# Ten dk stores that leave out one DMA engine, in place of eight that leave out two

## The chip, the core and the metric

The kernel runs on one core of a Trainium2 chip. The time is that of one launch on the device in microseconds (us), median of several runs. A ratio of two kernels is of their fast runs (in brackets its 95% interval); it isn't quite the ratio of the medians that stand beside it. The kernel before was timed anew in each set of rounds: 1280.82 to 1284.12 us median, single runs 1278.9 to 1287.4. The first four experiments ran on one chip and the other eight on another; where the text compares kernels of the two, the kernel before differs by 1.5 us between them (1280.82 and 1282.27).

## The reference

Attention of one query row per head, forward and backward: 64 heads (2 x 32), 8192 keys, head width 128, bf16.

```python
def _fwd_reference(q, k, v):
    scale = q.shape[-1] ** -0.5
    scores = jnp.einsum("bhqd,bhkd->bhqk", q, k) * scale
    p = _softmax(scores, axis=-1)
    return jnp.einsum("bhqk,bhkd->bhqd", p, v)
# outputs: out, and by jax.vjp of it with grad_out: dq, dk, dv
```

k and v are 134 MB each and are read once; dk and dv have the same size and are written once. That is 537 MB of traffic in some 1.28 ms, so it is a kernel of the DMA engines.

## The kernel before

A head's k or v is one tile of 128 partitions, 16 KB each, taken from twelve slots. It is loaded by SyncE, used, overwritten in place by dk or dv on VectorE, and stored by GpSimd. Of the 64 dk stores, eight are "spread": split by rows into 126 and 2.

```python
NTILE = 12
FIRST = 6
SPREAD = range(4, 60, 7)
...
    def by_rows(eng, dst, src, rows):
        p = 0
        for m in rows:
            pin(eng.dma_start(out=dst[p : p + m], in_=src[p : p + m], max_dma_last_dim=NT * D))
            p += m
...
        r0 = FIRST if w == 0 else 0        # GpSimd loads the first 6 rows of q
        if r0:
            pin(store_eng.inc_swdge_sem([], [], mode="reset_dge_cursor"))
            pin(store_eng.dma_start(out=qd_nat[:r0, w, :], in_=rows[:r0], max_dma_last_dim=D))
        pin(load_eng.dma_start(out=qd_nat[r0:BH, w, :], in_=rows[r0:BH]))
...
            if w == 0 and i in SPREAD:
                by_rows(store_eng, dst, h.tile[w], (P - 2, 2))
            else:
                eng = load_eng if len(ends) > 1 else store_eng
                pin(eng.dma_start(out=dst[:, b0:b1, :], in_=h.tile[w][:, b0:b1, :]))
...
        load_eng.dma_start(out=dst.rearrange("b h s d -> (b h s) d"), in_=nat[:BH, 0, :])
```

The load of 6 rows sets the cursor from which GpSimd's next narrower DMA takes its engines. 126 rows run on 14 engines, from 6 around to 3; the 2 rows then run on 4 and 5, and the cursor is at 6 again.

## Time and profile before

| | |
|---|---|
| median of the first three runs | 1284.47 us (1283.77 to 1285.12) |
| span of the profiled run | 1284.2 us |
| DMA packet time of loads and stores | 98.7% of 16 engines' span |
| plateau of traffic | 428 GB/s |

GpSimd's store issues, from the page's last part (engine, operation, count, KB of one, us from issue to landing):

```profile
out_dram<-kvt POOLq DMA_DIRECT2D x118, 2048.0 KB, 51.5
...
out_dram<-kvt POOLq DMA_DIRECT2D x8, 2016.0 KB, 55.7
...
out_dram<-kvt POOLq DMA_DIRECT2D x8, 32.0 KB, 55.2
```

A store is 2 MB and takes 51.5 us to land, while loads and stores of such tiles follow each other every 9.7 us: about five stores are under way at once.

### The profile page before, as it was taken

Reading aid. Unit: us, or ns where it says so; the run is one execution under the profiler, and the core shown is the slowest. Engines: PE = TensorE matmul, PEld = TensorE weight load, DVE = VectorE, ACT = ScalarE, POOL = GpSimd, SP = SyncE. Lnnn points to the kernel's source line nnn. Section 1 sums busy time; section 2 is a strip of 40 time slices with the busy share of each in tenths; the row PEclk is TensorE's granted clock in tenths of the full one; section 3 lists DMA queues with packets and bytes.
Section 4 is the critical chain, followed back from the end, with each engine's and each line's share of the span. In section 5 each row is a group of like instructions: output and inputs, shape, how many; then the busy total and the mean of one; then the engine's idle time right before and its main releaser. Section 6 shows DMA issues by size and latency. Waiting matters only on the chain.

```text
span 1284.2 us, 32475 instructions
## 1 busy us (share of the span) xinstructions
PE 1099.4 (86%) x14148; PEld 805.5 (63%) x14148; DVE 1014.6 (79%) x2258; ACT 956.9 (75%) x641; POOL 76.0 (6%) x143
## 2 busy tenths in 40 slices
PE   6899899899889899889899889888888799879870
PEld 5666666666666666666666666666656566656650
DVE  2888888888888888888888888888788688777882
ACT  6777777778778778778778778777778687777750
POOL 0000000000000000000000000000000000000000
PEclk9999999999999999999999999999999899999985
DMA  9999999999999999999999999999999999999995
GB/s 388 427 428 428 428 429 428 427 428 428 428 428 428 420 428 428 428 424 426 428 428 418 425 428 428 422 418 426 428 427 419 422 429 429 426 423 429 428 413 219
DMA packets 40155, 539.03 MB, mean 420 GB/s; under 512 B 5196, under 2 KB 5196, under 8 KB 6476
## 3 DMA queue, kind: packets, MB, share of 16 engines
q1 hardware_dynamic: 20172, 272.70, 49.9%
q0 software_dynamic: 19840, 264.25, 48.8%
q8 instruction: 110, 1.80, 0.5%
q14 instruction: 33, 0.27, 0.1%
HBM read 268.47 MB, written 268.47 MB: 418 GB/s over the span
## 4 chain that ended last, share of the span: by engine, by line
DVE 32%; DMA 17%; issue 14%; another core or an unknown queue 14%; PE 12%; ACT 8%; POOL 1%; SPq 0%; ACTq 0%; POOLq 0%; DVEq 0%
DVE kvt L427 18%; DMA kvt<-in_v_dram 11%; ACT ev L196 8%; PE tp L194 7%; DMA out_dram<-kvt 6%; DVE sel L395 4%; DVE rows L221 3%; DVE sel L389 1%; PE acc L372 1%; DVE pair L303 1%; PE raw L208 1%; ACT E_f L271 1%; DVE dSu L349 1%; PE sw L178 1%
## 5 line engine op out<-in xcount | busy, mean ns | idle before, releaser
L196 ACT COPY ev<-tp 128x2048 bf16<-128x2048 bf16 x512 | 941.3, 1868 | 285.7 <-PE tp L194 280.6
L427 DVE TENSOR_TENSOR kvt<-qb,pair 128x2048 bf16<-128x2048 bf16 x512 | 616.9, 1216 | 0.1
L194 PEld LDWEIGHTS <-kvt 128*128 128x128 bf16 x8192 | 507.0, 102 | 160.7 <-issue 114.4
L194 PE MATMUL tp<-ident_bf,kvt 128*128 128x128 bf16 x8192 | 572.9, 226 | 38.0 <-DMA kvt<-in_v_dram 28.8
L208 PE MATMUL raw<-ev,qdT 128*32 128x512 bf16 x2048 | 210.0, 399 | 5.0 <-ACT ev L196 1.6
L395 DVE SCALAR_TENSOR_TENSOR sel<-acc,diag,sel 128x128 f32<-128x128 f32 x384 | 134.7, 351 | 13.6
L228 PEld LDWEIGHTS sw<-sel,rows 128*128 128x128 f32 x1024 | 124.8, 192 | 29.7 <-issue 12.9
L228 PE MATMUL sw<-sel,rows 128*128 128x16 f32 x1024 | 137.2, 266 | 0.6 <-DVE rl L324 0.6
L372 PE MATMUL acc<-kvt,E_pad 128*32 128x512 bf16 x1024 | 102.9, 391 | 30.6 <-DVE E_pad L280 30.6
L445 POOL DMA_DIRECT2D out_dram<-kvt x118 | 63.3, 536 | 1081.9 <-DVE kvt L427 518.1
L372 PE MATMUL acc<-kvt,dS_pad 128*32 128x512 bf16 x1024 | 111.1, 426 | 0.8 <-DVE dS_pad L358 0.8
L221 DVE COPY rows<-raw 128x512 f32<-128x512 f32 x128 | 87.5, 684 | 26.1 <-PE raw L208 26.1
L178 PE MATMUL sw<-ident_bf,qdT 128*128 128x128 bf16 x128 | 28.5, 223 | 70.9 <-DVE mp L240 70.8
L280 DVE CAST E_pad<-E_f 128x64 bf16<-128x64 f32 x64 | 12.5, 195 | 92.9 <-ACT E_f L271 92.9
L208 PEld LDWEIGHTS <-qdT 128*32 128x32 bf16 x2048 | 64.6, 95 | 25.0 <-issue 18.4
L315 PEld LDWEIGHTS sw<-ld,ones 128*128 128x128 f32 x256 | 38.2, 188 | 54.5 <-issue 29.3
L372 PEld LDWEIGHTS <-E_pad 128*32 128x32 bf16 x1024 | 26.3, 93 | 55.2 <-DVE E_pad L280 40.1
L246 DVE TENSOR_REDUCE gm<-sw 1x1 f32<-1x128 f32 x64 | 17.9, 279 | 49.3 <-PE sw L244 49.3
L409 PE MATMUL acc<-ones,sel 128*128 128x1 f32 x256 | 47.5, 255 | 6.2 <-DVE sel L395 6.2
L315 PE MATMUL sw<-ld,ones 128*128 128x1 f32 x256 | 49.1, 261 | 0.1
L409 PEld LDWEIGHTS acc<-ones,sel 128*128 128x128 f32 x256 | 44.0, 215 | 7.3 <-DVE sel L395 7.3
L389 DVE TENSOR_SCALAR sel<-acc,diag 128x128 f32<-128x128 f32 x128 | 43.8, 342 | 0.0
(49 smaller groups left out, 367.5 us busy)
## 6 DMA issues: line engine op xcount, KB each, us to landing
out_dram<-kvt POOLq DMA_DIRECT2D x118, 2048.0 KB, 51.5
kvt<-in_v_dram SPq DMA_DIRECT2D x64, 2048.0 KB, 19.1
kvt<-in_k_dram SPq DMA_DIRECT2D x63, 2048.0 KB, 19.4
out_dram<-kvt POOLq DMA_DIRECT2D x8, 2016.0 KB, 55.7
out_dram<-kvt SPq DMA_DIRECT2D x8, 512.0 KB, 23.2
kvt<-in_k_dram SPq DMA_DIRECT2D x2, 512.0 KB, 4.5
kvt<-in_k_dram SPq DMA_DIRECT2D x1, 1024.0 KB, 7.2
out_dram<-kvt POOLq DMA_DIRECT2D x8, 32.0 KB, 55.2
```

The costliest lines, as they stand in the source:

```text
L194: pin(nc.tensor.transpose(tp[:, t, :], src[:, c * CH + t, :], ident_bf[:]))
L196: pin(nc.scalar.copy(out=ev[:], in_=tp[:]))
L208: nc.tensor.matmul(h.raw[g * SW : (g + 1) * SW, :], lhsT=qdT[:, w, q0 : q0 + SW], rhs=ev[:, g * QT : (g + 1) * QT, :].rearrange("p n d -> ...
L221: pin(nc.vector.tensor_copy(out=h.rows[:], in_=h.raw[:]))
L228: nc.tensor.matmul(h.score[w].rearrange("p (n t) -> p n t", t=QT)[:, :, t], lhsT=h.rows[:, t * P : (t + 1) * P], rhs=sel4[:].rearrange("p ...
L315: nc.tensor.matmul(out, lhsT=ones[:].to_broadcast([P, P]), rhs=col, start=True, stop=True)
L372: nc.tensor.matmul(h.acc[w][g : g + CW, :], lhsT=wts[:, n0 : n0 + CW], rhs=rows[:, n0 : n0 + QT, :].rearrange("p n d -> p (n d)"), start=( ...
L389: nc.vector.tensor_scalar(out=h.sel[:], in0=block, scalar1=diag[:, 0:1], scalar2=None, op0=ALU.mult)
L395: nc.vector.scalar_tensor_tensor(out=h.sel[:], in0=block, scalar=diag[:, b : b + 1], in1=h.sel[:], op0=ALU.mult, op1=ALU.add,)
L409: nc.tensor.matmul(h.acc[w][:, 0:1], lhsT=h.sel[:], rhs=ones[:], start=True, stop=True)
L427: nc.vector.tensor_tensor(out=h.tile[w][:, n0 : n0 + CH, :].rearrange("p n (e t) -> p n e t", t=2), in0=h.qb[w][:] .rearrange("p (e t) -> ...
L445: pin(eng.dma_start(out=dst[:, b0:b1, :], in_=h.tile[w][:, b0:b1, :]))
```

## The change

The intent is a better balance of the 16 DMA engines. Engine 4 gets its rows back, engine 5 is relieved more, and the rest of each spread store is dealt out so that the cursor returns to 6. The two small outputs at the end go out in five pieces on fewer engines.

```diff
-SPREAD = range(4, 60, 7)
+SPREAD = range(4, 60, 6)
@@
-                by_rows(store_eng, dst, h.tile[w], (P - 2, 2))
+                by_rows(store_eng, dst, h.tile[w], (P - 8, 5))
+                for b in range(NCH):
+                    r = (slice(P - 3, P), slice(b * CH, (b + 1) * CH))
+                    pin(
+                        store_eng.dma_start(
+                            out=dst[r], in_=h.tile[w][r], max_dma_last_dim=CH * D
+                        )
+                    )
@@
-        load_eng.dma_start(out=dst.rearrange("b h s d -> (b h s) d"), in_=nat[:BH, 0, :])
+        rows = dst.rearrange("b h s d -> (b h s) d")
+        p = 0
+        for m in (5, 44, 15) if w == 0 else (39, 25):
+            load_eng.dma_start(out=rows[p : p + m], in_=nat[p : p + m, 0, :], max_dma_last_dim=D)
+            p += m
```

## The prediction

> **What bounds the kernel now.** I read the page first: the engines' shares, the slices, the queues, then the issues.
>
> ```profile
> PE 1099.4 (86%) x14148; PEld 805.5 (63%) x14148; DVE 1014.6 (79%) x2258; ACT 956.9 (75%) x641; POOL 76.0 (6%) x143
> ...
> DMA  9999999999999999999999999999999999999995
> GB/s 388 427 428 428 428 429 428 427 428 428 428 428 428 420 428 428 428 424 426 428 428 418 425 428 428 422 418 426 428 427 419 422 429 429 426 423 429 428 413 219
> ...
> q1 hardware_dynamic: 20172, 272.70, 49.9%
> q0 software_dynamic: 19840, 264.25, 48.8%
> q8 instruction: 110, 1.80, 0.5%
> q14 instruction: 33, 0.27, 0.1%
> HBM read 268.47 MB, written 268.47 MB: 418 GB/s over the span
> ```
>
> The slices show the DMA engines at 90% or more until the last slice, at a plateau of 428 GB/s. No compute engine is over 86%. Loads (q1) and stores (q0) take 98.7% of the packet time. So the time is that of the 16 DMA engines, above all of whichever finishes last. Who waits agrees. First SyncE's queue, which issues the loads, then GpSimd, which issues the stores:
>
> ```profile
> SPq L100 <- DMA out_dram<-kvt: 1138.7, 116, 25.0
> ```
>
> ```profile
> POOL out_dram L445 <- DVE kvt L427: 518.1, 51, 14.6
> POOL out_dram L445 <- DVE qb L187: 438.0, 55, 32.3
> POOL out_dram L445 <- DMA out_dram<-kvt: 89.2, 9, 14.1
> ```
>
> Nearly every load waits 1138.7 us in all for the store of the tile that it overwrites. A store has landed when the last of 16 engines has landed its share. Next, the end, in stretches (length, busy time of PE, PEld, DVE, ACT, POOL, clock, DMA share, GB/s):
>
> ```profile
> 1258.00:1263.00 5.00, 0.90 (x3) 0.63 (x3) 2.82 (x8) 0.00 (x0) 0.00 (x0) 0.50 0.95 396
> 1263.00:1272.00 9.00, 0.00 (x0) 0.00 (x0) 0.00 (x0) 0.00 (x0) 0.00 (x0) 0.50 0.56 232
> 1272.00:1278.00 6.00, 0.00 (x0) 0.00 (x0) 0.00 (x0) 0.00 (x0) 0.00 (x0) 0.50 0.19 76
> 1278.00:1284.20 6.20, 0.00 (x0) 0.00 (x0) 0.00 (x0) 0.00 (x0) 0.00 (x0) 0.50 0.05 18
> ```
>
> Compute is over at 1263 us. After that engines run dry one by one: 56% busy, then 19%, then 5%, about one engine of 16. The sixteen landings of the last 4-KB-per-row dk store spread the same way: 1262.2 us plus 0, 0, 0, 0, 0.2, 3.3, 3.9, 5.3, 10.1, 10.6, 11.6, 11.7, 12.1, 12.2, 14.2 and 20.2 us. The mean is 7.2, so perfect sharing would end about 13 us sooner (20.2 - 7.2), and one engine alone costs 6 us (20.2 - 14.2). The most that rebalancing can give is therefore about 1%.
>
> **Who is late and why.** The packet records do not name the engine, but a 16-KB packet takes 611 ns and the next on that engine starts 607 ns after it, so I strung the packets into 16 chains by end and start; nearly all fit within 2 ns. From the chains:
> - The 110 fetches of q8 (16 KB, mean 963 ns) rotate over eight engines, 13 or 14 each. One delays its engine by 1.35 us, some 18.9 us for 14.
> - One engine is slower all the time: 1,700 of its 16-KB packets take 3 to 100 ns more, 42.3 us in the run, evenly spread. It has no q8 fetch.
> - The two engines that get no rows of the 126-row stores (4 and 5) are this slow one and one of the eight fetching ones. I cannot read from the trace which number belongs to which, but the diff keeps relief for 5 alone, so I take 5 as the slow one.
> - From the third spread store on, stretches of packets take about twice their time (800 to 1,400 ns) in the 20 to 40 us after each 126-row store is issued. Apart from fetches, such stalls cost the last engine 10.2 us, the fetching one of the pair 16.1 us (8 of them on loads), the other fetching engines 0 to 3.
>
> **What the Trainium skill says.** "DMA: Bandwidth & Descriptors", section "Why a DMA increments its semaphore by 16 and not by 1": a DMA runs on the largest k up to 16 that divides its slowest dimension; from GpSimd the k engines are consecutive from a round-robin cursor. It also reports direct copies spread over 16 with the rows rounded up. The trace agrees with the first rule: each 126-row store put 18 packets of 8 KB on 14 chains and none on two, which then got the 2 rows. The same page, "The descriptor swizzle": a 128-partition transfer puts fixed partitions on fixed engines; a store by consecutive rows breaks that pairing, which would suit the stalls, but no view here proves it. The same page, "Where 436 GB/s comes from": 435 GB/s for 16 ports, 27.2 each; the trace has 16384 B / 607 ns = 27.0. Its section "Latency and other measured facts" calls engines 7 and 15 usually slower; here the steadily slow one is in the pair 4 and 5.
>
> **The change part by part.** A row (16 KB) costs an engine 0.607 us. Against 8 rows each:
> - Before, eight stores: engines 4 and 5 get 1 row, 56 fewer in all (-34.0 us); the others 9, 8 more (+4.9 us).
> - After, ten stores. 120 rows on 15 engines are 8 each, skipping 5. The cursor is then at 5: five rows go to 5 to 9, one each. The four quarters of three rows go to 10-12, 13-15, 0-2 and 3-5, a quarter row each. Engine 5 has 1.25 rows, 67.5 fewer over ten stores (-41.0 us); 6 to 9 have 9 (+6.1 us); 0-4 and 10-15 have 8.25 (+1.5 us). The cursor is back at 6.
>
> So against before, engines 0-3 and 10-15 lose 5.5 rows (-3.3 us), 6 to 9 gain 2 (+1.2 us), 5 loses 11.5 (-7.0 us), and 4 gains 58.5 (+35.5 us).
>
> Sums over a clean engine, and where each ends on the trace's clock, with the last engine's 34.0 set at 1282.4:
> - The last engine before: 18.9 fetches + 4.9 rows + 10.2 stalls = 34.0. After: 30.6 if it is one of 10 to 15 (ends 1279.0), 35.2 if one of 6 to 9 (1283.6).
> - Other fetching engines before: 24 to 27, which fits their landings 8 to 10 us sooner. After: 20 to 23, or 25 to 28 among 6 to 9 (1273 to 1276).
> - Engine 4 (fetching) before: 18.9 - 34.0 + 16.1 = 1. After: 36.5 with all its stalls (1284.9). Its 8 us on loads I put down to its running ahead with nothing queued, which should go: then 28.4 (1276.8).
> - Engine 5: 42.3 - 34.0 = 8.3 before, 1.3 after.
>
> Ten spread stores for eight may add a quarter to the stalls, 2.5 us on a 10-us engine. The end is the maximum over engines. I expect 1278 to 1283 for the last landing, then 1.7 us as before (1284.47 against 1282.8): 1280 to 1285. I lean to 1282.
>
> Beside other work and free: 40 more GpSimd issues at some 0.6 us each (24 us on an engine that is 6% busy), 160 small packets per ten stores more, and three more output stores at the end (five for two, 256-byte rows of about 15 ns). The last of these are issued within about 3 us of 1266, long before the last engine is done, so they add nothing while the tail is over 10 us.
>
> **Rivals.**
> - *GpSimd's completion slots become the bound.* Store completions use eight semaphores in turn; a spread store takes six instead of two, so the next large store waits for the landing of the second store before it. A store takes 51.5 us to land and one is ready every 9.7 us, so that wait is about 51.5 - 29 = 22 us, ten times: the 89.2 us above would become 200 to 500. For it: the wait exists already. Against: at that moment the slowest engine still has two stores queued, some 19 us of work shared with loads, so only engines that are ahead go idle. If I am wrong, some us per spread store are lost: 1295 to 1310.
> - *Engine 4 becomes the last.* It loses all its relief. With its stalls kept and a quarter more of them, it ends at 1289 or so, and the time is 1291. For: it had the most stalls. Against: being 20 us and more ahead was part of them.
> - *Balance works well.* With the stalls gone, the last engine is a fetching one among 6 to 9, 25 over a clean engine: ends at 1273.4, time 1275.
> - *120 rows run on 16 engines rounded up (8 rows on 0 to 14).* Then 5 keeps its 42.3 us unrelieved, the time is about 1292, and 15 is idle early. Against: 126 rows did not do so.
>
> **Range and chances.** The best case is about 1271 (perfect sharing), so a gain of 2% (1258.8) is out of reach; a loss of 2% (1310) needs the first rival in full. Main case 1280 to 1285, engine 4 or slots to 1291, good balance to 1275: 1282, range 1274 to 1291. Faster 0.01, same 0.97, slower 0.02.
>
> **What would show it.** Right: plateau of 428 GB/s unchanged, q8 still 110 fetches; the 120-row stores as packets on 15 chains, one chain with few; a tail with several engines ending together and a smaller spread than 20.2 us if the time falls. The formerly early engine of the pair should land among the fetching ones. GpSimd's waits on its own stores should rise several times without a dip in the GB/s slices. Wrong: slices well under 420 after each spread store (slots), or one chain alone at the end with 8 us on the rest (engine 4, or 5 if rounding up).

## The result

The changed kernel takes 1315.2 us median of four runs (1312.16 to 1319.15), against 1284.12 for the kernel before. The ratio is 1.0249 (95% interval 1.0213 to 1.0285): 31 us slower, where 2 us faster was predicted, and outside the range.

The same lines of the page, for the changed kernel:

```profile
PE 1112.1 (85%) x14148; PEld 814.2 (62%) x14148; DVE 1016.1 (77%) x2258; ACT 958.2 (73%) x641; POOL 100.1 (8%) x185
...
DMA  9999999999999999999999999999999999999986
GB/s 388 426 429 428 429 427 428 427 420 427 429 416 393 430 427 389 390 428 426 357 428 428 427 385 427 428 410 378 428 429 384 393 428 425 365 428 428 413 371 280
...
q1 hardware_dynamic: 20317, 272.70, 49.3%
q0 software_dynamic: 21216, 264.26, 48.2%
q8 instruction: 110, 1.80, 0.5%
```

The plateau is still 428 GB/s and the bytes are the same. From the ninth slice on, though, the traffic falls again and again, down to 357. The lost time lies in these dips. Each dip comes some 30 to 80 us after a spread store is issued: the one that belongs to the store of 582 us lies between 625 and 651 us. The two kernels in that stretch (columns as in the prediction), before and after:

```profile
625.00:651.00 26.00, 22.75 (x313) 16.84 (x310) 23.36 (x52) 20.90 (x14) 1.60 (x3) 1.00 1.01 428
```

```profile
625.00:651.00 26.00, 23.16 (x313) 16.83 (x314) 23.36 (x53) 22.14 (x14) 1.14 (x2) 1.00 0.93 373
```

GpSimd's waits, and the load queue's, after:

```profile
POOL out_dram L452 <- DVE kvt L427: 296.1, 30, 18.3
...
POOL out_dram L446 <- DMA out_dram<-kvt: 229.9, 28, 9.6
...
POOL out_dram L452 <- DMA out_dram<-kvt: 69.6, 6, 14.2
```

```profile
SPq L100 <- DMA out_dram<-kvt: 1166.1, 125, 25.8
```

GpSimd's waits for its own stores rise from 89.2 to 299.5 us (229.9 + 69.6); most of them sit in front of the quarter-row stores (L446), one at a time as slots come free. At first sight that is the prediction's first rival, the completion slots. The end of the run says otherwise:

```profile
1288.00:1299.00 11.00, 0.00 (x0) 0.00 (x0) 0.00 (x0) 0.00 (x0) 0.00 (x0) 0.50 0.99 414
1299.00:1304.00 5.00, 0.00 (x0) 0.00 (x0) 0.00 (x0) 0.00 (x0) 0.00 (x0) 0.50 0.95 374
1304.00:1312.50 8.50, 0.00 (x0) 0.00 (x0) 0.00 (x0) 0.00 (x0) 0.00 (x0) 0.50 0.08 28
```

Fifteen engines end together near 1304 us, and for 8.5 us one engine is alone (0.08 of 16 is 1.3). The sixteen landings of the last dk piece are at 0 to 1.4 us, and one at 8.6. The same holds inside the run: of the 120-row store issued at 1069.5 us, fifteen engines had landed within 4.7 us and the sixteenth 26.0 us after the first. In the kernel before, such landings were scattered evenly over 61 us.

Strung into chains as in the prediction, the packets show which engine that is. In the first spread store one chain has no row of the 120 and then two packets of the 5-row store: the engine that is left out, number 5. It is an engine that fetches instructions. The steadily slow chain has 16 packets of the 120 rows and its quarter row in the fourth quarter, so it is engine 3 or 4; the kernel before left out the slow chain and one more of 4 and 5, so it is **engine 4**. Over the run this chain has 1,248 packets that are 3 to 100 ns late (29.3 us) and 72 that are over 100 ns late (28.8 us), and it is never idle. Every other chain is idle for 17 to 34 us in all. (Where two chains start packets at the same time they can change places, so single numbers of the other fifteen are uncertain; the slow chain is marked by its packets.)

So the engine that lost its relief does bound the run, and the others wait for it: no load may overwrite a tile before its store has landed on all sixteen. What isn't settled by this trace is why it needs 20 us more than its packets' sum in the prediction, and whether the slots have a part.

### The profile page after: what moved, and what is told of

It is laid out like the page before. It is cut to its first block, busy times and chain, and to the rows that moved or that the text cites. A ratio compares the mean times of both kernels' runs of the same rounds, so it can differ in the third digit from the quotient of the medians.

```text
span 1315.0 us, 32556 instructions
## 1 busy us (share of the span) xinstructions
PE 1112.1 (85%) x14148; PEld 814.2 (62%) x14148; DVE 1016.1 (77%) x2258; ACT 958.2 (73%) x641; POOL 100.1 (8%) x185
## 2 busy tenths in 40 slices
DMA packets 41677, 539.04 MB, mean 410 GB/s; under 512 B 6401, under 2 KB 6401, under 8 KB 7801
## 4 chain that ended last, share of the span: by engine, by line
DVE 30%; DMA 25%; another core or an unknown queue 17%; PE 10%; ACT 8%; issue 6%; POOL 1%; SPq 0%; ACTq 0%; DVEq 0%; POOLq 0%
DVE kvt L427 17%; DMA out_dram<-kvt 14%; DMA kvt<-in_v_dram 9%; ACT ev L196 8%; PE tp L194 6%; DVE sel L395 4%; DVE rows L221 3%; DMA kvt<-in_k_dram 2%; DVE sel L389 1%; PE acc L372 1%; DVE pair L303 1%; PE raw L208 1%; ACT E_f L271 1%; DVE dSu L349 1%
## 5 line engine op out<-in xcount | busy, mean ns | idle before, releaser
L194 PE MATMUL tp<-ident_bf,kvt 128*128 128x128 bf16 x8192 | 580.6, 227 | 60.4 <-DMA kvt<-in_v_dram 47.6
L194 PEld LDWEIGHTS <-kvt 128*128 128x128 bf16 x8192 | 513.6, 103 | 179.7 <-issue 109.0
L389 DVE TENSOR_SCALAR sel<-acc,diag 128x128 f32<-128x128 f32 x128 | 43.8, 342 | 0.0
```

The lines of the kernel that those rows point to most:

```text
L194: pin(nc.tensor.transpose(tp[:, t, :], src[:, c * CH + t, :], ident_bf[:]))
L389: nc.vector.tensor_scalar(out=h.sel[:], in0=block, scalar1=diag[:, 0:1], scalar2=None, op0=ALU.mult)
```

## The experiments

Theory: engine 4 is the slow one, the change took its relief away, and the end of the run is the sum of its work. Rival: the six completion slots that each spread store takes. All twelve kernels gave correct results.

**Skip engine 4 in place of 5** (the changed kernel, one constant):

```diff
-FIRST = 6
+FIRST = 5
```

> The changed kernel with the first GpSimd load taking 5 rows in place of 6, so that the cursor stands one lower and every spread store skips engine 4 in place of 5; as many stores, rows and completion slots as the changed kernel. Theory (engine 4 is the steadily slow one, the change took its relief away and the end is the sum of its work): engine 4 loses 67.5 rows against 80 where it had gained 2.5, 70 x 0.607 = 42.5 us, so it is no longer last; a fetching engine is, and the time is 1270 to 1284, below the changed kernel by 30 us or more. Rival (GpSimd's completion slots): the slots are used up just as before, 1310 to 1320.

Measured: 1286.92 us (1285.08 to 1290.07), ratio 1.0047 to before. Of the 31 us, 28 are back (1315.2 - 1286.9; 26 by the ratios), with the same stores, sizes and slots. The trace agrees: the chain without a row of the first 120-row store is now the steadily slow one (from 118 to 200 us, 86% of its 16-KB packets are 3 to 100 ns late, at most 5% on any other). That settles which engine it was. The GB/s slices of the page:

```profile
GB/s 389 425 428 427 428 429 427 427 425 428 428 427 422 427 429 427 423 428 428 411 422 427 426 422 428 426 428 423 428 428 414 421 427 427 388 428 429 424 408 291
```

The dips to 357 to 393 are gone but for one of 388. GpSimd's waits for its own stores are nearly as long (248.3 us), so long waits there don't make the run slow:

```profile
POOL out_dram L446 <- DMA out_dram<-kvt: 172.9, 23, 10.6
POOL out_dram L452 <- DMA out_dram<-kvt: 75.4, 9, 13.7
```

The time missed the forecast of 1270 to 1284, though: this version doesn't beat the kernel before.

**Slots alone, on the kernel before:** after each spread store, the next dv store in five column pieces.

```diff
+            elif w == 1 and i - 1 in SPREAD:
+                for f0, f1 in ((0, 8), (8, 16), (16, 32), (32, 48), (48, 64)):
+                    pin(store_eng.dma_start(out=dst[:, f0:f1, :], in_=h.tile[w][:, f0:f1, :]))
```

> The kernel before, its rows as they were, but the dv store right after each of the eight spread stores cut into five column pieces of all 128 partitions: seven slots in a row in place of three, cursor and rows per engine unchanged. Theory: 1280 to 1290, as before, while GpSimd's waits on its own stores rise from 89 us to 200 or more. Rival (slots): 20 to 30 us slower, 1304 to 1314, with dips in the GB/s slices after each.

Measured: 1286.63 us (1280.19 to 1289.74), ratio 1.003 (0.9985 to 1.0074). GpSimd's waits, where L445 are the pieces:

```profile
POOL out_dram L445 <- DMA out_dram<-kvt: 136.2, 16, 13.2
POOL out_dram L448 <- DMA out_dram<-kvt: 90.4, 8, 14.3
```

The waits rise to 226.6 us as wanted and cost nothing that these rounds can tell from zero (the interval is -2 to 9 us). As the bound of this kernel, the slots are out.

**No spread store at all** (kernel before with `SPREAD = ()`):

> The kernel before without any spread store (all 128-row stores by GpSimd): engine 4 without relief, no extra slots, no misplaced rows. Theory: engine 4 has 42.3 us over a clean engine and ends the run; 1292 on the scale of the prediction, up to 1311 if the stalls that it had in the changed kernel come from being last and not from the misplaced rows; one engine alone late in the last stores, by 10 us or more. Rival (slots): with no slot wait at all the fetching engines bound it, 1268 to 1282.

Measured: 1293.77 us (1293.29 to 1294.27), ratio 1.0092. The page's slices, and the end of the run:

```profile
GB/s 388 426 429 429 430 427 428 428 429 428 428 428 428 428 430 429 427 429 428 428 429 428 428 429 428 429 429 429 428 426 425 415 428 420 428 416 428 415 291 208
```

```profile
1279.00:1284.00 5.00, 0.90 (x3) 0.63 (x3) 1.70 (x7) 0.00 (x0) 0.00 (x0) 0.50 0.52 209
1284.00:1291.00 7.00, 0.00 (x0) 0.00 (x0) 0.00 (x0) 0.00 (x0) 0.00 (x0) 0.50 0.07 26
```

The sum of the prediction, applied to the right engine, gives 42.3 us over a clean engine, hence 1292. The last dk piece lands within 0.6 us on fifteen engines and at 9.0 us on one. The plateau holds until the backlog of the fast engines is used up near the end. So an unrelieved engine 4 costs some 12 us as such (0.92%), and the changed kernel, which gives it 2.5 rows (1.5 us) more, must lose the other 20 us by something else in the spread stores.

**The output pieces alone** (the last part of the diff on the kernel before):

> The kernel before with only the last part of the change: the two small output stores in five pieces on fewer engines. Theory and rival alike: hidden behind the tail of the stores, 1280 to 1288. If the five issues held the end, it would be 3 to 10 us slower.

Measured: 1281.86 us (1278.37 to 1284.73), ratio 0.9998 (0.9958 to 1.0037). This part does nothing that these rounds can tell from zero (the interval is -5 to 5 us).

**Skip 5 with three DMAs per store:**

```diff
-                by_rows(store_eng, dst, h.tile[w], (P - 2, 2))      # SPREAD as in the change
+                pin(store_eng.inc_swdge_sem([], [], mode="reset_dge_cursor"))
+                by_rows(store_eng, dst, h.tile[w], (6, P - 8, 2))
```

> Ten spread stores that skip engine 5 with three DMAs in place of six: the cursor set to 0 before each, then 6 rows (engines 0 to 5), 120 rows (15 engines, not 5), 2 rows (5 and 6). Engine 4 has 9 rows, 10 more in all than without spreading; half the slots of the changed kernel. Theory (engine 4 last, without relief): slow as the changed kernel, within 10 us of it, 1305 to 1325. Rival (slots): most of the loss gone, under 1298.

Measured: 1313.08 us (1311.35 to 1314.75), ratio 1.0244. Half the slots, and the whole loss is there. GpSimd's waits for its own stores are 73.3 us, less than the 89.2 before, so here they can't be the cause:

```profile
POOL out_dram L446 <- DMA out_dram<-kvt: 36.8, 4, 13.1
POOL out_dram L89 <- DMA out_dram<-kvt: 36.5, 6, 9.2
```

The last dk piece lands on one engine alone at 24.9 us, on the next at 9.8. Engine 4 has 7.5 rows more than in the changed kernel (10 against 2.5, 4.6 us), so the two aren't quite alike, but the rival's 1298 is far off.

**Skip 4 with three DMAs per store** (rows 5, 120, 3):

> The same three DMAs, but 5 rows (engines 0 to 4), 120 rows (not 4), 3 rows (4, 5 and 6): engine 4 has 2 rows in each of ten, 60 fewer (-36.4 us), 0 to 3, 5 and 6 have 9. Theory: 1270 to 1284, 25 us or more below its twin that skips 5. Rival (slots): the same as its twin.

Measured: 1297.65 us median, but 1284.13, 1294.85, 1300.44 and 1300.52 in its four runs; ratio 1.0131. It is 15 us below its twin, so the theory has the direction right, but both of its figures are missed (25 us or more, 1270 to 1284). The profiled run was the fast one of 1284.13, so what happened in the others isn't seen; this stays open.

**Ten stores of 126 and 2 rows** (kernel before, step 6 in place of 7):

> The kernel before with ten spread stores of 126 and 2 rows in place of eight: engines 4 and 5 lose 14 more rows each (-8.5 us), all others gain 2 (+1.2 us), 4 slots more. Theory: the last is a fetching engine, 1.2 us and a little more in stalls later: 1283 to 1290. Rival (more spread stores are slow in themselves, each 3 us as in the changed kernel): 1290 or more.

Measured: 1288.16 us (1282.87 to 1293.18), ratio 1.0049 (1.0012 to 1.0087). Inside the theory's range, but the spread of the runs reaches into the rival's.

**The changed kernel with eight spread stores** (step 7):

> The changed kernel with eight spread stores in place of ten: engine 4 gets 2 rows over 80 in place of 2.5, so by rows alone nothing changes for it. Theory with stalls from the misplaced rows: a fifth of the some 26 us of stalls on engine 4 goes, 1307 to 1313. Rival (slots or misplaced rows carry the whole loss): a fifth of the 31 us goes as well, 1306 to 1312; so this is a dose only and does not tell the two apart. If the stalls come with being last: no change, 1312 to 1318.

Measured: 1304.71 us (1304.11 to 1305.41), ratio 1.0179. That is below all the forecasts. Two stores fewer take away 10.5 us, of which rows are 0.3 (half a row). So the extra loss belongs to the number of spread stores. It isn't in proportion: eight stores cost 10.9 us over no spread at all (1304.7 - 1293.8), ten cost 21.4.

**Six slots and nothing else** (no rows moved, ten dk stores in six column pieces):

```diff
-                by_rows(store_eng, dst, h.tile[w], (P - 2, 2))      # SPREAD as in the change
+                for f0, f1 in ((0, 8), (8, 16), (16, 24), (24, 32), (32, 48), (48, 64)):
+                    pin(store_eng.dma_start(out=dst[:, f0:f1, :], in_=h.tile[w][:, f0:f1, :]))
```

> No misplaced rows and no relief for any engine, but the ten dk stores of the changed kernel cut into six column pieces of all 128 partitions each: the six slots of the changed kernel and nothing else of it, engine 4 without relief and last. Without pieces (no spread at all) this measured 1293.8. Theory (the other 20 us come from rows read by other engines than usual while engine 4 has no reserve): 1292 to 1298. Rival (the slots jam GpSimd and cost the last engine some 2 us per store): 1305 to 1316.

Measured: 1299.01 us (1298.58 to 1300.78), ratio 1.0139. Just above the theory's range: with engine 4 last, the slots (and smaller packets) cost some 5 us over no spread at all.

```profile
POOL out_dram L443 <- DMA out_dram<-kvt: 210.9, 25, 9.9
```

**Rows read by other engines, and nothing else** (ten dk stores as two halves of 64 rows, `(P // 2, P // 2)`):

> The ten dk stores as two DMAs of 64 rows, four rows to each engine in each: 8 rows for everyone, no relief, one slot more, the cursor not moved, but the rows read by other engines than usual. Theory: dearer than no spread at all (1293.8) by the stalls, 1300 to 1315. Rival (slots or rows per engine): 1292 to 1297.

Measured: 1303.91 us (1299.98 to 1313.98), ratio 1.0185 (1.0136 to 1.0233). No relief for anyone, one more slot, 8 rows for each engine as before, and some 10 us over no spread at all. So splitting a store by rows costs time in itself, about 1 us per store here. GpSimd's waits for its own stores are only 14.1 us, so it isn't the slots. It is less clear who pays: in the profiled run the last dk piece lands within 3.8 us on twelve engines and at 12.6, 15.2, 20.8 and 21.7 us on four, so this isn't engine 4 alone.

**Two versions with fewer spread stores.** One is the version that skips engine 4 with six of them (`FIRST = 5`, step 10):

> The version that skips engine 4, with six spread stores in place of ten: engine 4 loses 40.5 rows (-24.6 us) and stands at 42.3 - 24.6 = 17.7 over a clean engine, as the fetching ones (18.9 + 0.9 to 3.6); fewer misplaced rows. Theory: 1273 to 1282, the best so far, 0 to 8 us below before. If the stalls don't fall with the number of spread stores: 1284 to 1288.

Measured: 1279.51 us (1276.78 to 1280.69), ratio 0.998 (0.9965 to 0.9995). The other is the kernel before with five stores of 126 and 2 rows (step 12):

> The kernel before with five spread stores of 126 and 2 rows in place of eight: engines 4 and 5 lose 35 rows (-21.2 us; engine 4 at 21.1, engine 5 at -2), the others gain 5 (+3.0 us; a fetching one at 21.9). Theory: 1273 to 1282 as the one above. If engine 4 with its smaller relief becomes the last with stalls: 1285 to 1292.

Measured: 1276.69 us (1275.47 to 1277.16), ratio 0.9959 (0.9946 to 0.9972). Both are inside the theory's range, and the second is the fastest kernel, 0.4% below the kernel before.

```profile
GB/s 390 425 429 429 427 427 428 428 428 426 431 426 428 428 429 428 428 428 428 418 427 427 429 428 428 429 425 427 429 427 429 429 428 427 428 429 427 430 422 292
```

It holds the plateau but for one slice of 418, and nine of the sixteen landings of its last dk piece come within 1.6 us (16.1 to 17.7).

## Why the prediction was wrong

**The step that failed** is in "Who is late and why": "I cannot read from the trace which number belongs to which, but the diff keeps relief for 5 alone, so I take 5 as the slow one." The slow engine is 4, and 5 is a fetching one. The identity was taken from the intent, not from the trace. The working already held the consequence: "4 gains 58.5 (+35.5 us)". With the slow engine as 4 its own sum is 42.3 + 1.5 = 43.8 over a clean engine, 9.8 above the 34.0 set at 1282.4: a last landing at 1292.2 and a time of 1293.9 instead of 1282. The kernel without spread stores, where that engine has 42.3, measured 1293.8.

**A term that was mis-sized** is the stalls, "a quarter to the stalls, 2.5 us on a 10-us engine". On engine 4 they are about 20 us: 1315.2, less the 1293.8 without spread stores, less 1.5 for rows. On its chain in the changed kernel, the packets over 100 ns late make up 28.8 us. With engine 4 without relief, six slots per store alone cost 5 us, and two halves alone 10 us. The kernel that skips 5 with three DMAs is closer to the change: without long slot waits it loses 13 us besides rows (1313.1 - 1293.8, less 6.1 for ten rows). Slots and split rows so account for some 18 of the 20 us, as an estimate from these sums over two chips; how the loss divides is not shown. In the kernel before, engine 4 was among the first to be done at the end and had four packets over 100 ns late, against 72 after. Why a packet takes twice its time is open.

**The rivals.** "Engine 4 becomes the last" named the right number, for a wrong reason: it was thought the fetching engine, and its 1291 lacked the slow packets. The sign that it named, one chain alone at the end, came (8.5 us). For the slots, the wait came as foretold ("would become 200 to 500": 299.5 us), and so did the dips that were to show it. They were no proof: dips come wherever fifteen engines wait for one. What told them apart was the chain without idle time, then one constant, and then the kernel with the whole loss and short slot waits. "120 rows run on 16 engines rounded up" is out: the trace has 15 chains with 16 packets and one without. "Balance works well" needed engine 4 relieved.

**What held.** The engines bound the run, with the plateau unchanged and 110 fetches. The rows per engine came out as worked out, packet for packet, for five rows and quarter rows too. The output pieces cost nothing that shows. The sum of an engine's work gave 1292 for a kernel that took 1293.8, and forecast both faster versions within their ranges. It is no more than a first estimate, though: skipping 4 in ten stores missed the forecast of 1270 to 1284 in both forms (1286.92 and 1297.65), and eight stores came out below theirs.

**Slips that changed nothing.** The 98.7% is a share of the 16 engines' span, not of the packet time. The "160 small packets" more are 1,522 packets in all (41,677 - 40,155), most of them of 4 or 8 bytes and about 9 ns each. A packet of 256 bytes takes 18 ns, not 15. The "27.2 each" is an estimate, the page's 435 over 16.

## What to carry to other kernels

In this kernel, bound by sixteen DMA engines, the time followed the largest of sixteen sums, and a store that all must finish made the others wait for that one. So find out which engine is late before moving work, and prove its number by a run that moves one constant, never by the intent of a diff. Splitting a store has a price (with engine 4 unrelieved, some 1 us for two halves, 2 us for the changed kernel's six parts), so give just as much relief as makes the late engines level, in as few stores as possible.

## What the Trainium skill lacked or had wrong

- "DMA: Bandwidth & Descriptors", section "Latency and other measured facts", names engines 7 and 15 as usually slower. Here it is engine 4, as numbered by the cursor: 1,628 (1,700 as the prediction strung the packets) of its 16-KB packets before and 1,248 after are 3 to 100 ns late, 40.0 and 29.3 us, and no other chain of these two runs has over 4 us of such. No run shows why.
- The same page, "Why a DMA increments its semaphore by 16 and not by 1", gives the rule for the engines and the cursor, and the traces agree. It lacks that an engine without a share gets as many tiny packets as the others have real ones: 380 extra packets of 4 bytes in the ten 120-row and 5-row stores (10 x (16 + 11 x 2)), and 520 of 8 bytes for the quarter rows (10 x 4 x 13).
- The same page, "Rules for kernel authors", has no cost for a store split by rows: ten stores in two halves of 64 rows took some 10 us more than none (1303.91 against 1293.77).
- "Runtime: NRT & Kernel Launch", section "Instruction fetch mechanics", has no figure for what the fetch of instructions costs the DMA engines: 110 fetches of 16 KB on q8, on eight of the engines in turn, mean 963 ns, each delaying its engine by about 1.35 us.
